# Pooled attention with mixture-of-adapters: another order for the first batch's keys and scores

## The chip, the cores and the metric

The kernel runs on one core of a Trainium2 chip. The core has five engines that run side by side, each through its own list of instructions in order: TensorE (PE) multiplies matrices and transposes tiles, and writes its results to PSUM; VectorE (DVE), ScalarE (ACT) and GpSimd (POOL) work element by element; SyncE (SP) issues transfers (DMAs). An engine that needs another's result waits on a semaphore, and what stands behind the waiting instruction waits too. The metric is the device time of one execution in microseconds (us). The kernel before takes 426.56 us (median of 8 runs, 426.06 to 428.17).

## The reference

There are four batches, each with 12288 queries of 128 channels and a map of 384 x 32 x 128. The map is averaged over patches of 4 x 4 and projected, which gives 768 keys, used as the values too. Each query attends over them. Each row of the result goes through two of eight small adapters, weighted by a softmax over its two largest gate logits, and the sum is added to it.

```python
kv_pool = kv.reshape(B, H // r, r, W // r, r, C).mean(axis=(2, 4))
k = v = kv_pool.reshape(B, -1, C) @ w_sr
s = scale * (q @ k.transpose(0, 2, 1))
a = softmax(s)
x = a @ v                          # 49152 rows of 128
logits = x @ w_gate                # 8 experts, the best two kept
out = x + sum_e w_e * ((x @ A[e]) @ B[e])
```

## The kernel before

**Tiles.** Queries are taken in chunks of 512 (`T`), numbered 0 to 95 over all batches; four chunks make a group of 2048 (`GC`, `GT`). A batch's 768 keys are six tiles of 128 (`J`), treated as three key blocks of two tiles each (`h` or `r` = 0, 1, 2). For each chunk `k` and key block `r`, `scores(k, r)` (L238) multiplies the two key tiles with the chunk's transposed queries (512 columns each) into one of two PSUM buffers (`ps_s`, tile `sg`), and ScalarE takes the exponential of both at once, 128 x 1024 (L246, tile `em`). `attend(k, s)` (L248) multiplies the exponentials with the values (`vx`, which carry the gate's logits and a column of ones beside the 128 channels) into `acc`: 24 matmuls for a chunk. `normalize`, `top`, `route`, `gates`, `transposes`, `down`, `gate`, `up` and `finish` do the rest for a chunk, and `finish` stores it.

**The loop.** From step `k` = 4 (`LA`, L422) on, each step computes the scores of chunk `k`, attends for earlier chunks (table `att`) and passes still earlier ones through the adapters. The next batch's map is loaded and pooled meanwhile, with the additions on GpSimd (L171). Query groups 2 and later are cast to bf16 by a transfer from POOL's queue (`cast_q`) and loaded transposed (`load_qT`, issued by SP).

**The head.** Before the loop stands what the first batch needs (L372 to L390): its keys and values, and the scores of chunks 0 to 3. Query groups 0 and 1 are loaded as they are and transposed on TensorE, four pieces of 128 x 128 to a chunk (`turn_q`, L107), and copied out by ScalarE (L116). A block of the map is loaded in eight pieces of 256 KB: rows `r` = 0 to 3 of the patches, and two halves `x` (each half becomes one key tile). DVE adds rows 0 and 1 and rows 2 and 3 (`pair_step`, L173, recorded as L175). The rest of the sum is made by TensorE: 16 transposes of 128 x 128 accumulate in PSUM (`keys`, L187, tile `kpT_ps`). DVE scales them out (L200, `kpT`), TensorE projects (`keys2`, tile `kfT_ps`) and DVE copies the keys out (L207, `kfT`). `values` (L209) projects the same `kpT` to the values, copied by DVE (L216).

**What sets the order.** The order on every engine is the order in the program's text, as all calls are wrapped in `keep`. Transposes, projections and values share two PSUM buffers (`ps_m`). SP issues all loads in order: the 1 MB of query group 0, then the 24 pieces of the map, then query group 1 in four pieces and the adapters' matrices. On POOL the casts of the query groups 2 and 3 wait for the last piece of group 1 (`late`, L393). In the head TensorE gets: all 16 query transposes of group 0; block 0's keys; scores (0,0) and (1,0); then for each further block its transposes, scores of chunks 2 and 3 with the block before, the projection, the values of the block before, and scores of chunks 0 and 1 with the new block. The last scores are (2,2) and (3,2); then come the first four query transposes of group 1 (L400) and, as the loop's first work, attention of chunk 0 (L448) and scores (4,0).

Every matrix instruction goes through the helper `mm` and so is recorded as L68; the tiles' names tell them apart.

Of the kernel before, what the change touches and what calls it, by code (L numbers as in the profile page):

```python
# [20 lines left out]
def kernel(  # L21
# [10 lines left out]
    nc = tc.nc  # L32
# [92 lines left out]
    load_q(0, 0, GC * S)  # L125
    for h in range(3):
        for r in range(4):
            for x in range(2):
                load_kv(0, h, r, x)
    for m in range(GC):  # L130
        load_q(1, m * S, m * S + S)
# [26 lines left out]
    def prepare(b, adder):  # L158
# [3 lines left out]
        def pool_step(h, step, lo, hi):  # L162
# [3 lines left out]
            else:  # L166
                w = 2 * C if step == 3 else C
                u, v = t[:, 0, :, 0:w], t[:, 0, :, w:2 * w]
                keep(adder.tensor_tensor(u, u, v, op=ALU.add))
                return  # L170
            keep(adder.tensor_tensor(u[:, lo:hi], u[:, lo:hi], v[:, lo:hi], op=ALU.add))  # L171

        def pair_step(h, r, x):  # L173
            u, v = (kvr[b, h][:, r + i, x] for i in range(2))
            keep(adder.tensor_tensor(u, u, v, op=ALU.add))  # L175

        for h in range(3):
            if adder is nc.vector:
                sums.append([lambda h=h, r=r, x=x: pair_step(h, r, x)
                             for r in (0, 2) for x in range(2)])  # L180
                continue
            sums.append([lambda h=h, step=step, lo=lo: pool_step(h, step, lo, lo + 512)
                         for step in range(5) for lo in range(0, 1024 if step < 3 else 512, 512)])
# [3 lines left out]
        def keys(h):  # L187
# [5 lines left out]
            if adder is nc.vector:  # L193
                parts = [(r, i, c) for r in (0, 2) for i in range(2) for c in range(4)]
            else:
                parts = [(0, i, 0) for i in range(2)]
            for n, (r, i, c) in enumerate(parts):
                mm(ps[:, i], kvr[b, h][:, r, i, c * C:(c + 1) * C], id_f, is_transpose=True,
                   start=(n == 0), stop=(n == len(parts) - 1))
# [3 lines left out]
        def keys2(h):  # L203
            kpT = st["kpT"]
            ps = mtile([P, 2, P], name="kfT_ps")
            mm(ps, w_sr_sb, kpT[:, 2 * h:2 * h + 2], start=True, stop=True)
            keep(nc.vector.tensor_copy(kfT[b][:, 2 * h:2 * h + 2], ps))  # L207

        def values(h):  # L209
            if h == 0:  # L210
                vx[b] = per_b.tile([P, J, VE], FP16, tag="vx", name="vx")
                keep(nc.vector.memset(vx[b][:, :, VC:VE], 1.0))
            ps = mtile([P, 2, VC], name="v_ps")
            for i in range(2):
                mm(ps[:, i], st["kpT"][:, 2 * h + i], wext, start=(i == 0), stop=(i == 1))
            keep(nc.vector.tensor_copy(vx[b][:, 2 * h:2 * h + 2, 0:VC], ps))  # L216
            if adder is not nc.vector:
                st["vb", h] = prep.tile([P, 2, C], BF16, tag="vb", name="vb")
                keep(nc.vector.tensor_copy(st["vb", h], ps[:, :, 0:C]))
# [8 lines left out]
        for h in range(3):  # L228
            for f in (keys, keys2, values) if adder is nc.vector else (keys, values, turn):
# [142 lines left out]
    for m in range(GC):  # L372
        turn_q(0, m, nc.scalar)
    sums, rest = prepare(0, nc.vector)
    for h in range(3):
        for item in sums[h]:
            item()
        rest[3 * h]()
        if h > 0:
            scores(2, h - 1)  # L380
        rest[3 * h + 1]()
        if h > 0:
            scores(3, h - 1)
            rest[3 * h - 1]()
        scores(0, h)
        scores(1, h)
    rest[8]()
    scores(2, 2)
    scores(3, 2)
    rest = []  # L390
# [31 lines left out]
    for k in range(LA, last + 3):  # L422
# [10 lines left out]
        if b + 1 < B:  # L433
            if i == 4:
                sums, rest = prepare(b + 1, nc.gpsimd)
# [99 lines left out]
```

The softmax here doesn't subtract the row's maximum and nothing guards it: scores larger than these inputs give would overflow.

## Time and profile before

| | |
|---|---|
| median of 8 runs | 426.56 us (426.06 to 428.17) |
| the profiled execution | 425.39 us, of which the profile's span is 423.3 us |
| TensorE busy | 389.5 us, 92% of the span |
| VectorE, ScalarE, GpSimd busy | 327.3, 292.9 and 162.5 us |
| first exponential of the head | starts at 15.24 us |
| first exponential of loop step 4 | starts at 31.57 us |
| ScalarE's exponentials | 288 of 1.02 us each |
| mean rate of the DMAs | 181 GB/s; 393 to 397 GB/s from 6 to 24 us |

How to read it: the page gives for each engine its busy time and its share of the span, then the span in 40 slices with a digit for the busy tenths of each. The chain of work that ended last is followed back from the last instruction, at each step to what released it, and its time is shared out by engine. The timeline lists instructions in order of time with start and length in us from the start of the span, `xN` where N alike ones were merged (the length is then that of all of them), and in brackets how long the engine was idle before and what ended that. Matmuls overlap: the next starts before the last has drained.

### The profile page before, as it was taken

To read this page: it belongs to the slowest core of one execution; us is meant where nothing else is said; L and a number is where in the kernel's file an instruction comes from. 1 tells how busy PE (TensorE), PEld (TensorE's weight loads), DVE (VectorE), ACT (ScalarE), POOL (GpSimd) and SP (SyncE) were. 2 spreads that over 40 slices of the span, in tenths; PEclk is the share of its full clock that TensorE was granted. 3 is DMA by queue.
4 is the path that set the end of the run, shared out by engine and by line. 5 is a ranking of instruction groups with operands and counts; after the bars stand their busy time and mean duration, and the time that the engine had idled before them with its cause. 6 is when DMAs were issued, how large, how long until landed. Compare 5 with 4: busy or idle time off the path is not lost.

```text
span 423.3 us, 11396 instructions
## 1 busy us (share of the span) xinstructions
PE 389.5 (92%) x4589; PEld 309.8 (73%) x4589; DVE 327.3 (77%) x967; ACT 292.9 (69%) x336; POOL 162.5 (38%) x263
## 2 busy tenths in 40 slices
PE   4898999999999999999999999999999998999843
PEld 3566777787877878787888778777888877788642
DVE  2644778788988878779888878779888888888853
ACT  3478567686777777676787777676777866678522
POOL 0010357965320557964330467963231312222000
PEclk9999999999999999999999999999999999999975
DMA  8989657776547999976547999966584628341112
GB/s 302 404 207 265 136 174 204 272 160 141 130 120 158 286 229 296 294 162 129 145 122 149 316 245 223 323 149 148 128 172 129 150 76 153 131 118 74 53 60 91
DMA packets 71172, 76.43 MB, mean 181 GB/s; under 512 B 49904, under 2 KB 50160, under 8 KB 70640
## 3 DMA queue, kind: packets, MB, share of 16 engines
q1 hardware_dynamic: 70128, 64.11, 52.2%
q0 software_dynamic: 704, 11.54, 15.4%
q8 instruction: 36, 0.59, 0.6%
q14 instruction: 16, 0.13, 0.1%
q10 hardware_dynamic: 288, 0.07, 0.1%
HBM read 50.53 MB, written 36.70 MB: 206 GB/s over the span
## 4 chain that ended last, share of the span: by engine, by line
PE 72%; DVE 10%; POOL 8%; ACT 3%; DMA 2%; issue 2%; SPq 1%; DVEq 0%; ACTq 0%
PE acc L68 28%; PE sg L68 23%; PE tt_ps L68 9%; PE h_ps L68 4%; PE d_ps L68 4%; POOL kvr L171 4%; DVE hg L350 3%; ACT em L246 2%; DVE osb L363 2%; DVE xn L263 2%; POOL over L293 1%; PE v_ps L68 1%; DMA kvr<-in_kv_dram 1%; DMA qf<-in_q_dram 1%; SPq L98 1%
## 5 line engine op out<-in xcount | busy, mean ns | idle before, releaser
L246 ACT ACTIVATE em<-sg 128x1024 f16<-128x1024 f32 x288 | 280.5, 1023 | 97.3 <-PE sg L68 96.4
L68 PE MATMUL acc<-vx,em 128*128 128x137 f16 x2304 | 174.5, 225 | 2.0 <-DVE xn L263 1.9
L68 PE MATMUL sg<-qT,kfT 128*128 128x512 bf16 x576 | 170.9, 378 | 2.7 <-ACT em L246 2.2
L68 PEld LDWEIGHTS <-em 128*128 128x128 f16 x2304 | 150.3, 98 | 4.9 <-DVE xn L263 2.2
L68 PEld LDWEIGHTS <-tts 128*128 128x128 bf16 x768 | 58.7, 99 | 53.1 <-ACT tts L334 5.5
L350 DVE TENSOR_TENSOR hg<-h_ps,gw 128x512 bf16<-128x512 f32 x96 | 66.1, 689 | 29.9 <-POOL gw L315 16.1
L293 POOL TENSOR_TENSOR over<-xn,srt 128x128 f32<-128x128 f32 (+1 forms) x54 | 19.7, 384 | 175.7 <-DVE srt L281 175.7
L263 DVE TENSOR_TENSOR xn<-acc,rinv 128x544 f32<-128x544 f32 x96 | 69.6, 725 | 3.3
L171 POOL TENSOR_TENSOR kvr<-kvr 128x512 f32<-128x512 f32 x54 | 67.4, 1268 | 2.1 <-PE d_ps L68 1.9
L363 DVE TENSOR_TENSOR osb<-d_ps,xn 128x512 f32<-128x512 f32 x96 | 65.9, 690 | 2.6 <-PE d_ps L68 2.6
L336 DVE COPY tts<-tt_ps 128x1024 bf16<-128x1024 bf16 (+1 forms) x95 | 64.0, 673 | 2.4 <-PE tt_ps L68 2.4
L68 PEld LDWEIGHTS <-xn 128*128 128x128 bf16 x384 | 29.5, 99 | 28.5 <-issue 6.1
L68 PEld LDWEIGHTS <-kfT 128*128 128x128 bf16 x576 | 45.9, 97 | 6.0 <-issue 3.7
L68 PE MATMUL h_ps<-a_bf,tts 128*128 128x128 bf16 x384 | 37.6, 221 | 6.1 <-ACT tts L334 3.9
L68 PE MATMUL tt_ps<-id_bf,xn 128*128 128x128 bf16 x384 | 37.4, 220 | 6.1 <-DVE hg L350 4.4
L258 DVE RECIPROCAL rinv<-acc 128x4 f32<-128x4 f32 x96 | 17.4, 181 | 32.8 <-PE acc L68 32.1
L68 PE MATMUL tt_ps<-id_bf,hg 128*128 128x128 bf16 x384 | 37.9, 222 | 3.2 <-DVE hg L350 2.8
L68 PE MATMUL d_ps<-b_bf,tts 128*128 128x128 bf16 x384 | 37.6, 222 | 2.8 <-DVE hg L350 1.2
L281 DVE MAX8 srt<-xn 128x8 f32<-128x8 f32 x384 | 34.6, 153 | 0.2
L68 PEld LDWEIGHTS <-hg 128*128 128x128 bf16 x384 | 25.9, 99 | 4.2 <-DVE hg L350 3.7
L312 ACT ACTIVATE th<-over 128x128 f32<-128x128 f32 (+2 forms) x33 | 9.1, 276 | 15.2 <-DVE over L298 11.8
L314 POOL TENSOR_TENSOR gw<-th,over 128x128 f32<-128x128 f32 (+1 forms) x27 | 11.0, 407 | 21.6 <-ACT th L312 21.5
(49 smaller groups left out, 164.5 us busy)
## 6 DMA issues: line engine op xcount, KB each, us to landing
out_dram<-osb SPq DMA_DIRECT2D x96, 256.0 KB, 3.4
kvr<-in_kv_dram SPq DMA_DIRECT2D x36, 512.0 KB, 6.6
qbf<-in_q_dram POOLq DMA_DIRECT2D x22, 512.0 KB, 7.2
kvr<-in_kv_dram SPq DMA_DIRECT2D x24, 256.0 KB, 5.1
qf<-in_q_dram SPq DMA_DIRECT2D x1, 1024.0 KB, 5.1
qf<-in_q_dram SPq DMA_DIRECT2D x4, 256.0 KB, 5.2
qT<-qbf SPq DMA_TRANSPOSE x22, 8.3
w_sr_sb<-in_w_sr_dram ACTq DMA_DIRECT2D x1, 64.0 KB, 4.0
```

Source lines behind the costliest of these rows:

```text
L68: return keep(nc.tensor.matmul(*a, **k))
L171: keep(adder.tensor_tensor(u[:, lo:hi], u[:, lo:hi], v[:, lo:hi], op=ALU.add))
L246: keep(nc.scalar.activation(em[k][:, 2 * r:2 * r + 2], ps, AF.Exp, bias=0.0, scale=scale))
L258: keep(nc.vector.reciprocal(ri, acc[k][:, :, VC]))
L263: keep(nc.vector.tensor_tensor(x, acc[k][:, :, 0:VC], ri.unsqueeze(2).broadcast_to([P, S, VC]), op=ALU.mult))
L281: keep(nc.vector.max(srt[k0][:, m, s], xn[k][:, s, C:VC]))
L293: keep(eng.tensor_tensor(d, lg, so[:, :, i].unsqueeze(2).broadcast_to([P, n, 8]), op=ALU.subtract))
L312: keep(nc.scalar.activation(th, arg, AF.Tanh, bias=0.0, scale=0.5))
L314: keep(eng.tensor_tensor(w[:, 0:n], th, mask, op=ALU.mult))
L336: keep(nc.vector.tensor_copy(sb[:, lo:hi], ps[:, lo:hi]))
L350: keep(nc.vector.tensor_tensor(hg[k].rearrange("p s (e r) -> p (s e) r", e=E), hp[k].rearrange("p s (e r) -> p (s e) r", e=E), gw[k0][:, m ...
L363: keep(nc.vector.tensor_tensor(osb, dp[k], xn[k][:, :, 0:C], op=ALU.add))
```

## The change

The loop is left as it is. What changes is the head. Query group 0 is loaded in two halves of 512 KB, with the eight pieces of block 0 between them. The pieces of each block are loaded half by half (`x` outside, `r` inside). The scores are taken block by block: all four chunks with block 0, then with block 1, then with block 2. Query chunks 2 and 3 are transposed between the scores of block 0. Block 2 is built in two columns, one key tile each, with scores of chunks 2 and 3 of block 1 between them; in its second column rows 2 and 3 aren't added by DVE, but both transposed into the sum by TensorE (four transposes more, one addition less). The attention of chunk 0 moves from the loop's first step to a place ahead of scores (3,2). `prepare` loses its branches for the first batch; for the other batches it does what it did.

```diff
-    load_q(0, 0, GC * S)
+    load_q(0, 0, 2 * S)
     for h in range(3):
-        for r in range(4):
-            for x in range(2):
+        for x in range(2):
+            for r in range(4):
                 load_kv(0, h, r, x)
+        if h == 0:
+            load_q(0, 2 * S, 4 * S)
...
+    def values_of(b, h, kpT):
...
+        ps = mtile([P, 2, VC], name="v_ps")
+        for i in range(2):
+            mm(ps[:, i], kpT[:, 2 * h + i], wext, start=(i == 0), stop=(i == 1))
+        keep(nc.vector.tensor_copy(vx[b][:, 2 * h:2 * h + 2, 0:VC], ps))
+        return ps
...
-    for m in range(GC):
-        turn_q(0, m, nc.scalar)
-    sums, rest = prepare(0, nc.vector)
-    for h in range(3):
-        for item in sums[h]:
-            item()
-        rest[3 * h]()
-        if h > 0:
-            scores(2, h - 1)
-        rest[3 * h + 1]()
-        if h > 0:
-            scores(3, h - 1)
-            rest[3 * h - 1]()
-        scores(0, h)
-        scores(1, h)
-    rest[8]()
-    scores(2, 2)
-    scores(3, 2)
-    rest = []
+    def pair(h, x, r):
+        u, v = (kvr[0, h][:, r + i, x] for i in range(2))
+        keep(nc.vector.tensor_tensor(u, u, v, op=ALU.add))
+
+    def patches(ps, h, x, rs, first_, last_):
+        n = [(r, c) for r in rs for c in range(4)]
+        for i, (r, c) in enumerate(n):
+            mm(ps, kvr[0, h][:, r, x, c * C:(c + 1) * C], id_f, is_transpose=True,
+               start=(first_ and i == 0), stop=(last_ and i == len(n) - 1))
+
+    def pooled(ps, lo, hi):
+        keep(nc.vector.tensor_scalar(kpT0[:, lo:hi], ps, 1.0 / 16.0, None, op0=ALU.mult))
+
+    def project(lo, hi):
+        ps = mtile([P, 2, P], name="kfT_ps")[:, 0:hi - lo]
+        mm(ps, w_sr_sb, kpT0[:, lo:hi], start=True, stop=True)
+        keep(nc.vector.tensor_copy(kfT[0][:, lo:hi], ps))
+
+    def both(h):
+        ps = mtile([P, 2, P], name="kpT_ps")
+        for x in range(2):
+            for r in (0, 2):
+                pair(h, x, r)
+                patches(ps[:, x], h, x, (r,), x == 0 and r == 0, x == 1 and r == 2)
+        pooled(ps, 2 * h, 2 * h + 2)
+        project(2 * h, 2 * h + 2)
+
+    turn_q(0, 0, nc.scalar)
+    turn_q(0, 1, nc.scalar)
+    both(0)
+    scores(0, 0)
+    scores(1, 0)
+    values_of(0, 0, kpT0)
+    turn_q(0, 2, nc.scalar)
+    scores(2, 0)
+    turn_q(0, 3, nc.scalar)
+    scores(3, 0)
+    both(1)
+    scores(0, 1)
+    scores(1, 1)
+    pair(2, 0, 0)
+    pair(2, 0, 2)
+    ps = mtile([P, P], name="kpT_ps")
+    patches(ps, 2, 0, (0, 2), True, True)
+    pooled(ps, 4, 5)
+    scores(2, 1)
+    values_of(0, 1, kpT0)
+    project(4, 5)
+    scores(3, 1)
+    pair(2, 1, 0)
+    ps = mtile([P, P], name="kpT_ps")
+    patches(ps, 2, 1, (0, 2, 3), True, True)
+    pooled(ps, 5, 6)
+    project(5, 6)
+    scores(0, 2)
+    scores(1, 2)
+    values_of(0, 2, kpT0)
+    scores(2, 2)
+    for s in range(S):
+        attend(0, s)
+    scores(3, 2)
...
         if k == LA:
-            for s in range(S):
-                attend(0, s)
             ka = []
```

## The prediction

> **What bounds the kernel now.** I read the page first (busy shares, slices, chain), then the timeline of the first 50 us, where the change lies, then the waits. The page:
>
> ```profile
> PE 389.5 (92%) x4589; PEld 309.8 (73%) x4589; DVE 327.3 (77%) x967; ACT 292.9 (69%) x336; POOL 162.5 (38%) x263
> ...
> PE   4898999999999999999999999999999998999843
> ...
> PE 72%; DVE 10%; POOL 8%; ACT 3%; DMA 2%; issue 2%; SPq 1%; DVEq 0%; ACTq 0%
> ...
> kvr<-in_kv_dram SPq DMA_DIRECT2D x24, 256.0 KB, 5.1
> qf<-in_q_dram SPq DMA_DIRECT2D x1, 1024.0 KB, 5.1
> ```
>
> TensorE is full except in the first slices and the last, and carries 72% of the chain. So what the head (the first batch's keys, up to the loop) gains or loses goes on to the end one for one, if nothing later stands at a fixed time. The head, in the timeline (start, length, engine, line, what; in brackets the idle time before it and who ended it):
>
> ```profile
> 6.52 3.74 PE L68 MATMUL qT_ps<-id_f,qf 128*128 128x128 f32 x16
> ...
> 10.69 1.41 DVE L175 TENSOR_TENSOR kvr<-kvr 128x512 f32<-128x512 f32 x2 [1.18 <-DMA kvr<-in_kv_dram]
> 12.84 0.43 DVE L200 TENSOR_SCALAR kpT<-kpT_ps 128x256 f32<-128x256 f32 x1 [0.75 <-PE kpT_ps L68]
> ...
> 14.12 0.42 DVE L207 CAST kfT<-kfT_ps 128x256 bf16<-128x256 f32 x1 [0.85 <-PE kfT_ps L68]
> ...
> 14.60 1.04 PE L68 MATMUL sg<-qT,kfT 128*128 128x512 bf16 x4 [0.52 <-DVE kfT L207]
> 15.24 1.94 ACT L246 ACTIVATE em<-sg 128x1024 f16<-128x1024 f32 x2 [4.36 <-PE sg L68]
> ...
> 15.47 1.04 PE L68 MATMUL kpT_ps<-id_f,kvr 128*128 128x128 f32 x8
> 16.10 1.47 DVE L175 TENSOR_TENSOR kvr<-kvr 128x512 f32<-128x512 f32 x2 [0.36 <-DMA kvr<-in_kv_dram]
> ...
> 18.32 0.42 DVE L200 TENSOR_SCALAR kpT<-kpT_ps 128x256 f32<-128x256 f32 x1 [0.75 <-PE kpT_ps L68]
> ...
> 19.97 2.85 ACT L246 ACTIVATE em<-sg 128x1024 f16<-128x1024 f32 x3 [0.19 <-PE sg L68]
> ```
>
> and its end:
>
> ```profile
> 25.67 4.69 ACT L246 ACTIVATE em<-sg 128x1024 f16<-128x1024 f32 x5 [0.19 <-PE sg L68]
> ...
> 29.44 1.66 PE L68 MATMUL acc<-vx,em 128*128 128x137 f16 x24
> 30.21 0.63 ACT L116 CAST qT<-qT_ps 128x512 bf16<-128x512 f32 x1
> ...
> 30.94 0.59 PE L68 MATMUL sg<-qT,kfT 128*128 128x512 bf16 x2
> ...
> 31.57 1.02 ACT L246 ACTIVATE em<-sg 128x1024 f16<-128x1024 f32 x1 [0.73 <-PE sg L68]
> ```
>
> Key block 0 waits for its loads (DVE until 10.69). From 15 us on ScalarE's exponentials set the pace, 0.92 apart when nothing stops them. They stop where a key block isn't ready:
>
> ```profile
> ACT em L246 <- PE sg L68: 8.0, 5, 4.4
> ```
>
> (ScalarE's waits from 14 to 31 us: 8.0 us in five waits, of which 4.4 before the first exponential.) The mark that I carry through is the first exponential of step 4, the loop's first: it starts at 31.57. TensorE reaches its scores, 30.94, when the copy of 30.21 to 30.84 is done, since that copy holds the queries of step 4.
>
> **The change, step by step.** I write e(k,r) for the exponential of query chunk k and key block r. On each engine instructions run in order.
>
> *Loads.* Only half of the 1 MB of queries now lies ahead of block 0's eight loads. The DMAs move 405 GB/s in the windows from 8 us on: 0.52 MB is 1.3 us; at the 302 to 370 GB/s of 2 to 6 us it would be 1.4 to 1.7, and 1.0 is the least if SP's issues (0.60 each, L98) are what paces the first ones. I take 1.3. Block 0's last two additions end at 12.10 - 1.3 = 10.8. The second half goes behind block 0, so blocks 1 and 2 land as before, and SP issues one DMA more (0.40): the loads of the next query group and of the adapters are issued up to 0.4 later, but the bytes before them are the same. The POOL copy that waits for them (24.57), the casts behind it in POOL's queue and the transposing load behind those in SP's (30.52) stay, or slip by at most 0.4; the tile that they make is used at step 8, more than 20 us later, which hides it. Column by column, an addition now needs loads 1 and 2, then 3 and 4: it costs nothing, the last one decides.
>
> *Block 0.* TensorE turns 8 query pieces first, not 16: 6.52 + 8 x 0.23 = 8.4. The 16 transposes of the keys follow the additions. At 0.107 a start (15.47: 8 in 1.04) the last four end 0.75 after the last addition, 11.55; if all still run at 0.23 a start, as the row at 6.52 does, 8.4 + 3.7 = 12.1. I take 11.9. From that copy to the first exponential it is 15.24 - 12.84 = 2.4: e(0,0) at 14.3, a gain of 0.95.
>
> *Block-major scores.* Now TensorE's order is scores 0, scores 1, values, turn query chunk 2, scores 2, turn chunk 3, scores 3, and only then the transposes of block 1. ScalarE's is e(0,0) 14.3, e(1,0) 15.2, copy of chunk 2 at 16.1 to 16.7. Scores 2 wait for that copy: 16.75, and their exponential follows 0.63 later (30.94 to 31.57), 17.4. Chunk 3 is turned behind scores 2, so its copy stands behind e(2,0): 18.3 to 18.9; scores 3 at 18.95, e(3,0) at 19.6. All that while block 1's transposes are queued behind scores 2 and 3 on TensorE. They start at 18.95 + 0.43 = 19.4, though their additions are done by 17.8 (the values' copy of 0.45 moves ahead of them on DVE; it is covered by this wait). Sixteen of them and the drain take 2.0: kpT at 21.4, where it was 18.32. Plus 2.4: e(0,1) at 23.8, where it was 20.89. The gain of 0.95 has become a loss of 2.9. ScalarE is idle from 20.6.
>
> *Block 2 by columns, with the last rows on TensorE.* Two additions behind block 1's copy on DVE (from 23.1, 0.6 apart) end at 24.4; four transposes to 25.1; kpT, 128x128, costs 0.29 (the nearest row is L150's 128x128 copy, 0.29; ends 0.17 for 128x8 and 0.43 for 128x256). Scores (2,1), values, the half projection and scores (3,1) follow: e(3,1) at 26.8. On DVE the values' copy (26.05 to 26.5) and the half key copy come before the one addition left: 26.7 to 27.4. Then 12 transposes (8 of rows that are no longer added, 4 in place of an addition of 0.69) to 28.9, kpT 0.29, half projection 0.45 (ends 0.35, as the 136-column values matmuls run, and 0.70, the whole one), copy 0.29, scores: e(0,2) at 30.7. Before it was 25.67 + 0.92 = 26.6, so the loss is 4.1. The last loads land near 22 (two loads per 1.35 us after 16.1), so the additions that went are no wait that ended: nothing stands on them any more.
>
> *Attention moved up.* The 24 matmuls (1.5) now stand ahead of scores 3, not behind them. e(1,2) 31.6, e(2,2) 32.5, attention 32.2 to 33.7, scores (3,2) 33.7, e(3,2) 34.35 instead of 33.45: 0.9 more, since ScalarE has nothing else. Then as before the copy of step 4's queries (35.25), scores at 35.9 and e of step 4 at 36.5. Normalising chunk 0 moves less (+2.7), but its products sit in ScalarE's queue behind step 4 and gain nothing.
>
> *Sum:* -0.95 + 3.85 (block-major) + 1.2 (columns) + 0.8 (attention) = 36.5 - 31.57 = +4.9. The unknown prices (half load 0.4 either way, clock 0.3, five narrow operations 0.1 each) make it +3.7 to +6.1. The profiled execution took 425.39 (span 423.3 and 2.1 around it), so 430.3; the median of the runs, 426.56, is 1.2 above it, and gives 431.5. A difference under 0.2%, 0.9 us, can't be told from none.
>
> **The clock of the transposes.** The transposes at 6.52 start 0.23 apart and those at 15.47 about 0.11, with the granted clock at 1.00 in both windows, so something halves TensorE's rate that the clock row doesn't show. In the new order TensorE has 8 query transposes fewer early on and idles more between 12 and 30 us. What it does on the path there at full rate is 36 transposes (3.9), seven score pairs (3.0), projections (1.1) and the attention (1.5), 9.5 us; if the full rate came after the head, the loss would be 4.9 + 9.5 = 14.4 us. If it came by 15 us, in place of some 11.5, it would cost about 1.2 more, by 18 us about 2.2 more.
>
> The Trainium skill, "TensorE: Matmul & The Clock Gate", Part 1, says that the array runs at half rate until one window of about 3.4 us has been busy, and falls back after an idle one; that speaks against this change. Its Part 4 says that transposes do not count as such activity. The rows contradict Part 4: between 6.52 and 12.8 us only transposes ran, and they sped up. By Part 1, with the near unbroken transposes from 6.5 to 11.9, the sum stays at +4.9; by Part 4 the first half of the head would be at half rate and the sum 6 to 7.
>
> **The rivals.** *The clock comes later* (above): 432.7 to 433.7, at worst 441. For it: fewer early transposes, four TensorE pauses of 0.6 to 1.5 us. Against: additions and transposes keep TensorE at work until about 12.
>
> *The loop absorbs the delay.* If the loop's start stood at a fixed time, that of next batch's loads or of POOL's additions (POOL has 8% of the chain), up to 4.9 us would vanish and the time be 426.6, no change. It decides if that slack is 4.9 or more. Against: after 24.6 no wait on a DMA is in the list of waits; POOL waits for DVE (175.7 us), ScalarE and TensorE, which all move along.
>
> *The change does what its order aims at,* and ScalarE runs through: twelve exponentials and two copies from 14.3 give step 4 at 27.7, 3.9 earlier, 422.7. It decides if block 1's keys are turned by 18, that is if TensorE isn't held at scores 2 and 3. Against: both wait for copies that stand behind exponentials.
>
> **How the numbers follow.** Forecast, +3.7 to +5.5: 0.72. Clock later: 0.15. Absorbed: 0.07. ScalarE through: 0.06. Range 429.6 to 433.8: from 0.8 below the low end of the sum, for slack that takes a little of it, to the clock at 18 us; it leaves out the last two cases and the clock's far end. Faster 0.06 (ScalarE through), same 0.05 (absorbed in full), slower 0.89 (the rest, with 0.02 for absorbed in part).
>
> **What would show it.** Exponentials of block 0 at about 14.3, 15.2, 17.4 and 19.6 with two query copies between; block 1's kpT copy near 21.4; ScalarE idle some 3 us before e(0,1) and again before e(0,2); step 4's first exponential near 36.5; the rows from 50 us on the same, later. It is wrong if block 1's transposes start before 18, if transposes are still 0.2 apart after 15 us, or if the delay at 36 us is smaller at 100.

## The result, and the profile after

The changed kernel takes 432.08 us (median of 11 runs) and the kernel before 426.56 us; the ratio is 1.0131, with a 95% interval of 1.0113 to 1.0148. It is slower by about 5.5 us. The ratio and its interval leave out executions in a slower state that any of these kernels now and then falls into (one of the eleven, at 442.84 us; the other ten took 430.94 to 434.99). The profiled execution took 431.16 us with a span of 429.2, against 425.39 and 423.3 before: 5.8 us more.

The page of the changed kernel, with the lines that answer to those shown of before (busy time by engine, TensorE's slices, the granted clock by slice, the chain that ended last, the query load):

```profile
PE 390.7 (91%) x4595; PEld 311.2 (73%) x4595; DVE 327.1 (76%) x968; ACT 293.1 (68%) x336; POOL 162.7 (38%) x263
...
PE   4677999999999999999999999999999998999853
...
PEclk9999999999999999999999999999999999999955
...
PE 69%; DVE 10%; POOL 9%; DMA 5%; ACT 3%; issue 2%; SPq 1%; ACTq 0%; DVEq 0%
...
qf<-in_q_dram SPq DMA_DIRECT2D x2, 512.0 KB, 5.7
```

TensorE's work is the same within 1.2 us. Its slices 2 to 4 fell from 898 to 677: the time was lost in the head, as idle time of TensorE. The chain's share of DMA rose from 2% to 5%, but this is no wait: the chain is followed back at 26.74 from a copy on VectorE to the landing of the adapters' `a_f`, which that copy does not read, and VectorE was busy with the copy ahead of it until 26.83. ScalarE's timeline of the head shows where (start, length, idle time before in brackets):

```profile
14.82 1.94 ACT L233 ACTIVATE em<-sg 128x1024 f16<-128x1024 f32 x2 [5.65 <-PE sg L68]
16.65 0.59 ACT L116 CAST qT<-qT_ps 128x512 bf16<-128x512 f32 x1
17.92 1.02 ACT L233 ACTIVATE em<-sg 128x1024 f16<-128x1024 f32 x1 [0.68 <-PE sg L68]
18.84 0.58 ACT L116 CAST qT<-qT_ps 128x512 bf16<-128x512 f32 x1
20.10 1.02 ACT L233 ACTIVATE em<-sg 128x1024 f16<-128x1024 f32 x1 [0.68 <-PE sg L68]
24.18 3.88 ACT L233 ACTIVATE em<-sg 128x1024 f16<-128x1024 f32 x4 [3.06 <-PE sg L68]
30.95 2.85 ACT L233 ACTIVATE em<-sg 128x1024 f16<-128x1024 f32 x3 [2.89 <-PE sg L68]
34.58 1.02 ACT L233 ACTIVATE em<-sg 128x1024 f16<-128x1024 f32 x1 [0.77 <-PE sg L68]
35.50 0.58 ACT L116 CAST qT<-qT_ps 128x512 bf16<-128x512 f32 x1
36.76 1.02 ACT L233 ACTIVATE em<-sg 128x1024 f16<-128x1024 f32 x1 [0.68 <-PE sg L68]
```

Each of ScalarE's pauses is put down to scores of TensorE. The two copies in block 0 are followed by pauses of 0.68; before the first exponential of block 1 it waits 3.06, before that of block 2 2.89. The exponential of step 4 starts at 36.76, where it was 31.57: 5.19 later. From there every exponential up to step 94 stays 5.19 to 5.22 later, so the loop neither absorbs nor adds anything. Behind the last exponential 0.64 more is added, which makes the 5.86 between the two spans. The timeline of TensorE and VectorE of the changed kernel shows what holds block 1:

```profile
19.47 0.59 PE L68 MATMUL sg<-qT,kfT 128*128 128x512 bf16 x2 [1.15 <-ACT qT L116]
19.54 0.69 DVE L364 TENSOR_TENSOR kvr<-kvr 128x512 f32<-128x512 f32 x1 [0.61 <-DMA kvr<-in_kv_dram]
19.90 1.91 PE L68 MATMUL kpT_ps<-id_f,kvr 128*128 128x128 f32 x16
...
21.84 0.42 DVE L373 TENSOR_SCALAR kpT<-kpT_ps 128x256 f32<-128x256 f32 x1 [1.61 <-PE kpT_ps L68]
```

TensorE waits 1.15 us for a query copy, does scores (3,0), and only then, at 19.90, turns block 1's keys; the copy-out of `kpT` starts at 21.84, before it was 18.32. The last addition of block 1 too ends late, at 20.23 (19.54 + 0.69; before 17.57), but the transposes have 12 other pieces to turn until then.

### The profile page after: what moved, and what is told of

Same layout as the page of the kernel before. It is cut to its first block, busy times and chain, and to the rows that moved or that the text cites. A ratio compares the mean times of both kernels' runs of the same rounds, so it can differ in the third digit from the quotient of the medians.

```text
span 429.2 us, 11412 instructions
## 1 busy us (share of the span) xinstructions
PE 390.7 (91%) x4595; PEld 311.2 (73%) x4595; DVE 327.1 (76%) x968; ACT 293.1 (68%) x336; POOL 162.7 (38%) x263
## 4 chain that ended last, share of the span: by engine, by line
PE 69%; DVE 10%; POOL 9%; DMA 5%; ACT 3%; issue 2%; SPq 1%; ACTq 0%; DVEq 0%
PE acc L68 27%; PE sg L68 22%; PE tt_ps L68 8%; PE d_ps L68 4%; PE h_ps L68 4%; POOL kvr L183 4%; DMA kvr<-in_kv_dram 3%; DVE hg L337 3%; DVE osb L350 2%; POOL over L280 2%; DVE xn L250 2%; ACT em L233 2%; PE v_ps L68 1%; SPq L98 1%; DVE tts L323 1%
## 5 line engine op out<-in xcount | busy, mean ns | idle before, releaser
L301 POOL TENSOR_TENSOR gw<-th,over 128x128 f32<-128x128 f32 (+1 forms) x27 | 11.0, 406 | 21.6 <-ACT th L299 21.5
```

The costliest lines, as they stand in the source:

```text
L301: keep(eng.tensor_tensor(w[:, 0:n], th, mask, op=ALU.mult))
```

## The experiments

My theory was the sum of the prediction: block-major order, columns and attention each cost what their waits show, and the two query halves cost nothing by themselves. The rivals were that part of the loss is TensorE's clock, which the sparser order keeps or loses, or the loads, which the second half of the queries pushes back. All times below are medians; each ratio is to executions of the kernel before that were made beside it (their medians are 426.24 to 426.86).

| kernel | us | ratio to before, interval | step 4's exponential in its profile, later than 31.57 by |
|---|---|---|---|
| the changed kernel | 432.08 | 1.0131 (1.0113 to 1.0148) | 5.19 |
| `half_alone` | 428.18 | 1.0046 (1.0031 to 1.0062) | 3.34 |
| `halves_ahead` | 426.54 | 0.9996 (0.9979 to 1.0012) | 0.48 |
| `attend_back` | 431.03 | 1.0124 (1.0078 to 1.0171) | 8.2 |
| `block2_whole` | 430.82 | 1.0100 (1.0079 to 1.0120) | 6.47 |
| `dve_copies` | 431.78 | 1.0134 (1.0101 to 1.0166) | 6.56 |
| `after_warm` | 431.15 | 1.0108 (1.0093 to 1.0123) | 5.37 |
| `block2_whole_warm` | 430.00 | 1.0073 (1.0055 to 1.0090) | 4.16 |
| `dve_copies_warm` | 430.44 | 1.0089 (1.0073 to 1.0106) | 4.66 |
| `half_warm` | 428.62 | 1.0053 (1.0025 to 1.0081) | 3.62 |
| `before_warm` | 427.51 | 1.0037 (1.0020 to 1.0054) | 0.98 |
| `whole_first` | 430.12 | 1.0081 (1.0055 to 1.0107) | 3.68 |
| `between` | 426.44 | 0.9995 (0.9980 to 1.0011) | 0.31 |

The last column is of single executions. In `half_alone`, `attend_back`, `block2_whole` and `dve_copies` that execution ran part of the head at half the clock; the medians say more there.

### The halves alone

`half_alone` is the kernel before with the query load cut in two around block 0, and chunks 2 and 3 turned after the scores of block 0:

```diff
-    load_q(0, 0, GC * S)
+    load_q(0, 0, 2 * S)
...
+        if h == 0:
+            load_q(0, 2 * S, 4 * S)
...
-    for m in range(GC):
+    for m in range(2):
         turn_q(0, m, nc.scalar)
...
         scores(1, h)
+        if h == 0:
+            for m in range(2, GC):
+                turn_q(0, m, nc.scalar)
```

> The kernel before with one part of the change: the queries in two halves around block 0, query chunks 2 and 3 transposed behind the first two scores of block 0; the loads otherwise, the order of the scores, block 2 and the attention as before. My theory (the half load brings block 0 forward by about 0.5 to 1 us, but the later blocks still wait for their own loads): the first exponential near 14.3 to 14.8 instead of 15.24, step 4 at 31.6 within 0.6, time 426 to 427.2. Rival (the second half slows the loads of block 1 and 2, which in the changed kernel landed some 1.7 us later than before): block 1's last addition ends near 19 to 20 instead of 17.57, step 4 at 33 or later, time 427.8 to 429.

It is slower by 0.46%, 2.0 us, so "no change" fell, and the rival's time of 427.8 to 429 came true. But the rival's reason did not show: block 1's last addition ended at 18.09, not at 19 to 20. In its profile TensorE ran at the half rate until 20.4 us, which its timeline shows by the lengths:

```profile
15.30 1.89 PE L68 MATMUL sg<-qT,kfT 128*128 128x512 bf16 x4 [0.52 <-DVE kfT L209]
16.98 1.92 PE L68 MATMUL qT_ps<-id_f,qf 128*128 128x128 f32 x8
18.84 2.72 PE L68 MATMUL kpT_ps<-id_f,kvr 128*128 128x128 f32 x16
21.40 0.59 PE L68 MATMUL sg<-qT,kfT 128*128 128x512 bf16 x2
```

Four score matmuls take 1.89 at 15.30, where before they took 1.04. Its transposes of block 1 started at 18.84, behind the turned queries.

`halves_ahead` cuts the load too, but puts both halves ahead of the map:

```diff
-    load_q(0, 0, GC * S)
+    load_q(0, 0, 2 * S)
+    load_q(0, 2 * S, 4 * S)
```

> The kernel of before with the 1 MB of queries cut in the same two halves, both still ahead of block 0; nothing else. In the profiles with the second half behind block 0 it took 0.8 to 2.4 us to land where 0.52 MB at 405 GB/s take 1.3, and all later loads came 0.5 to 1.8 later. Theory A (halves of 4 KB a partition are slow themselves): the second half lands at 6.0 or later (before: all at 5.5), block 0's last addition ends after 12.4, step 4 later by as much, time 427 to 428. Theory B (a half is slow only among the pieces of the map): landing at 5.5 within 0.3 and time 426.6 within 0.5.

The medians tell no difference: two loads in place of one cost nothing that this measurement can tell. (In its profile block 0's last addition ended at 12.61, beyond the 12.4 of theory A; but so it did with one whole load, at 12.86 in `between` and 12.78 in `before_warm`.) So what costs in `half_alone` is where the second half goes, and what TensorE then does when.

### The attention of chunk 0

`attend_back` puts it back into the loop's first step:

```diff
     scores(2, 2)
-    for s in range(S):
-        attend(0, s)
     scores(3, 2)
...
         if k == LA:
+            for s in range(S):
+                attend(0, s)
             ka = []
```

> The changed kernel with the attention of chunk 0 back behind scores (3,2), where it was before. My theory: the exponential (3,2) follows (2,2) again without a pause (33.7 instead of 34.58), step 4 starts 0.8 earlier, near 36.0; time 0.8 below the changed kernel's, about 431.3. Rival (the attention has to be done anyway and only changes places): no difference, 432.1 within 0.3.

The median is 1.0 us below the changed kernel's, but the interval of its ratio holds the changed kernel's 1.0131, so the time alone does not settle it. The mechanism can be read directly. In ScalarE's timeline of `attend_back` the last four exponentials of the head run through:

```profile
34.79 3.77 ACT L233 ACTIVATE em<-sg 128x1024 f16<-128x1024 f32 x4 [2.89 <-PE sg L68]
...
39.77 1.02 ACT L233 ACTIVATE em<-sg 128x1024 f16<-128x1024 f32 x1 [0.73 <-PE sg L68]
```

They start about 0.92 apart, where the changed kernel has three, a pause of 0.77 and the fourth (30.95 and 34.58 above). From block 2's first exponential to that of step 4 it is 4.98 here, as before (26.59 to 31.57), and 5.81 in the changed kernel. The attention ahead of scores (3,2) costs these 0.83; every profile with it there has 5.80 or 5.81.

### Block 2 in two columns

`block2_whole` is the changed kernel with block 2 in one piece, in the order of before; `block2_whole_warm` is the same with transposes that feed nothing in the pauses (they are explained below).

```diff
-    pair(2, 0, 0)
-    pair(2, 0, 2)
-    ps = mtile([P, P], name="kpT_ps")
-    patches(ps, 2, 0, (0, 2), True, True)
-    pooled(ps, 4, 5)
+    ps = mtile([P, 2, P], name="kpT_ps")
+    for x in range(2):
+        for r in (0, 2):
+            pair(2, x, r)
+            patches(ps[:, x], 2, x, (r,), x == 0 and r == 0, x == 1 and r == 2)
+    pooled(ps, 4, 6)
     scores(2, 1)
-    values_of(0, 1, kpT0)
-    project(4, 5)
+    project(4, 6)
     scores(3, 1)
-    pair(2, 1, 0)
...
-    project(5, 6)
+    values_of(0, 1, kpT0)
     scores(0, 2)
```

> The changed kernel with block 2 built in one piece, in the order of before (four additions on VectorE, 16 transposes, scores (2,1), projection, scores (3,1), values, scores (0,2)); everything else as changed. My theory (the two columns cost 1.2 us because each goes through VectorE and TensorE by turns): exponential (0,2) at 29.4 instead of 30.95, step 4 near 35.3, time 1.2 to 1.5 lower, 430.6 to 430.9. Rival (four whole additions and the last loads hold it up instead, as the change's last rows on TensorE suppose): no gain or a loss, 432 to 433.

> The kernel with block 2 in one piece, with the extra transposes. My theory (two columns cost 1.2): time 1.2 to 1.5 below the changed kernel with the extra transposes, exponential (0,2) at 29.4 to 29.6. Rival (the 1.3 that the run without extra transposes was below the changed kernel came from the clock): within 0.4 of it.

Both are about 1.2 us below their counterparts with columns (430.82 against 432.08; 430.00 against 431.15). The interval of `block2_whole` overlaps that of the changed kernel, but the four runs of `block2_whole_warm` (429.03 to 430.30) all lie below the four of `after_warm` (430.71 to 431.73). ScalarE's timeline of `block2_whole_warm`, blocks 1 and 2:

```profile
24.91 1.94 ACT L240 ACTIVATE em<-sg 128x1024 f16<-128x1024 f32 x2 [3.06 <-PE sg L68]
27.79 1.02 ACT L240 ACTIVATE em<-sg 128x1024 f16<-128x1024 f32 x1 [0.94 <-PE sg L68]
29.01 3.77 ACT L240 ACTIVATE em<-sg 128x1024 f16<-128x1024 f32 x4 [0.19 <-PE sg L68]
```

In one piece, ScalarE waits 0.94 and 0.19 in the middle of block 1 and then runs on; with columns it does all four of block 1 without a pause and then waits 2.89. From the first exponential of block 1 to that of block 2 it is 6.77 with columns (24.18 to 30.95) and 5.02 in one piece (24.91 to 29.93, the second of the four at 29.01). Of these 1.75 step 4 gains 1.21 in this execution (4.16 late against 5.37 in `after_warm`), since its block 0 began 0.55 later.

### The query copies between the scores

`dve_copies` lets VectorE copy chunks 2 and 3 and turns both ahead of scores (2,0); `dve_copies_warm` is that with the filler.

```diff
-    turn_q(0, 2, nc.scalar)
+    turn_q(0, 2, nc.vector)
+    turn_q(0, 3, nc.vector)
     scores(2, 0)
-    turn_q(0, 3, nc.scalar)
     scores(3, 0)
```

> The changed kernel with the copies of query chunks 2 and 3 on VectorE instead of ScalarE, both chunks transposed ahead of scores (2,0). It takes away what scores (2,0) and (3,0) wait for, the copies behind the exponentials. My theory (that wait holds block 1's transposes): exponentials (2,0) and (3,0) at 17.4 and 18.3 instead of 17.92 and 20.10, block 1's transposes start at 17.8 instead of 19.9; block 1's kpT then follows its last addition (ended 20.24 in the changed kernel's profile) at 20.9 instead of 21.84, and the time falls by 0.9, to 431.2; if the loads come as early as before (last addition 17.6), by 2.5 to 3, to 429. Rival (block 1 is held by its loads alone, not by the order): kpT stays at 21.8, time 432 within 0.4.

> The kernel with the copies of query chunks 2 and 3 on VectorE, with the extra transposes. The run without them lost the clock (half from 12.8 to 19.7 us) and so tells little of the order. My theory (block 1's transposes are held by scores 2 and 3, which wait for copies behind exponentials): exponentials (2,0), (3,0) near 17.4 and 18.3, block 1's kpT 0.75 after its last addition, step 4 at 34.8 to 35.9, time 0.9 to 2 below the changed kernel with the extra transposes. Rival (block 1 is held by its loads): no more than 0.3 below it.

Without the filler it gains nothing that can be told (431.78). With it, it is 0.7 below `after_warm`, less than the 0.9 to 2 expected, and the two sets of four runs overlap. VectorE's timeline of `dve_copies_warm` tells why it is not more:

```profile
16.72 1.45 DVE L118 CAST qT<-qT_ps 128x512 bf16<-128x512 f32 x2
18.08 2.49 DVE L371 TENSOR_TENSOR kvr<-kvr 128x512 f32<-128x512 f32 x4
21.32 0.42 DVE L380 TENSOR_SCALAR kpT<-kpT_ps 128x256 f32<-128x256 f32 x1 [0.75 <-PE kpT_ps L68]
```

The four additions of block 1 now stand behind the copies on VectorE, and block 1's keys are out at 21.32 in place of 21.84: the wait moved from ScalarE's copies to VectorE's additions.

`whole_first` takes the copies out of the way on ScalarE itself: the queries are loaded whole, ahead of the map, and all four chunks are turned first. The block-major order stays, with nothing between the scores.

```diff
-    load_q(0, 0, 2 * S)
+    load_q(0, 0, 4 * S)
...
-        if h == 0:
-            load_q(0, 2 * S, 4 * S)
...
     turn_q(0, 1, nc.scalar)
+    turn_q(0, 2, nc.scalar)
+    turn_q(0, 3, nc.scalar)
     both(0)
...
-    turn_q(0, 2, nc.scalar)
     scores(2, 0)
-    turn_q(0, 3, nc.scalar)
     scores(3, 0)
```

> The changed kernel with the 1 MB of queries in one load ahead of block 0 and all 16 query transposes and their copies ahead of block 0's keys, as before; the column-wise loads, the block-major scores without copies between them, block 2 in columns and the early attention stay. My theory (most of the block-major loss comes from the two copies and transposes between the scores, the rest from block 1's transposes behind scores 2 and 3): first exponential at 15.2, exponentials 2 and 3 at 17.1 and 18.0, block 1's transposes start at 17.7, exponential (0,1) at 22.0 (changed kernel 24.18, before 20.89), step 4 at 34.6, time 429.4 to 429.9. Rival (the copies don't matter, block-major order alone does it): exponential (0,1) stays near 24 and the time near 431 to 432.

430.12 us, 2.0 below the changed kernel and a little above the 429.4 to 429.9 expected. ScalarE's timeline of `whole_first`, blocks 0 and 1:

```profile
15.85 3.77 ACT L231 ACTIVATE em<-sg 128x1024 f16<-128x1024 f32 x4 [4.40 <-PE sg L68]
22.68 3.88 ACT L231 ACTIVATE em<-sg 128x1024 f16<-128x1024 f32 x4 [3.06 <-PE kfT_ps L68]
```

From block 0's first exponential to block 1's it is 6.83 here, 9.36 in the changed kernel (14.82 to 24.18) and 5.65 before (15.24 to 20.89). So of the 3.71 that the block-major order lost there, 2.53 is the two copies standing among the exponentials, and 1.18 is the order of the blocks itself. (The loads of block 1 came earlier here too, but in the changed kernel its keys did not wait for them.) Where the 1.18 comes from, VectorE's timeline of `whole_first` shows:

```profile
17.10 2.49 DVE L362 TENSOR_TENSOR kvr<-kvr 128x512 f32<-128x512 f32 x4
```

The four additions of block 1 follow the copy of block 0's values (16.74 to 17.19), which waits for TensorE behind the scores. They end at 19.59, before at 17.57, though the last piece of the block had landed at 17.26. In the changed kernel the wait for the query copies covers this; without the copies it is the next wait. About 1.0 of the 2.53 is given back at the start, since block 0 begins at 15.85 and not at 14.82.

### The clock

`after_warm` is the changed kernel with transposes of the identity into an accumulator that nothing reads, 16 at the start and 2 to 8 in the pauses. They feed nothing and only keep TensorE at work:

```diff
+    def fill(n):
+        for _ in range(n):
+            mm(scratch[:, 0, 0:P], id_f, id_f, is_transpose=True, start=True, stop=True)
+
+    fill(16)
...
     turn_q(0, 2, nc.scalar)
+    fill(8)
     scores(2, 0)
     turn_q(0, 3, nc.scalar)
+    fill(8)
     scores(3, 0)
```

> The changed kernel with extra transposes of the identity into an unused accumulator, 16 ahead of everything else on TensorE and 2 to 8 in each of its pauses in the head; they feed nothing. It keeps TensorE busy and moves no other work. My theory (in a part of the executions of the changed kernel the clock falls back to half in the pauses of the head, and that is the distance of its median from its best runs): no granted clock of 0.5 before 400 us, step 4 at 36.8 or a little earlier, time 430.4 to 431.2 with a spread under 1 us, against 432.08 with 430.9 to 435.0. Rival (the spread comes from the loads): median and spread stay, 432 within 0.4.

Its median is 0.9 us below the changed kernel's (431.15 against 432.08), though it does more, and its four runs lie within about 1 us (430.71 to 431.73). But the intervals of the two ratios overlap, so the 0.9 is not secured. In its profile the clock is full from 10.21 us to 409.6, and step 4 is 5.37 late, filler included; the profile of the changed kernel kept the clock too and has 5.19. This is the price of the order with the clock out of the question.

What the clock adds where it is lost can be read from the distance between the first exponentials of block 0 and block 1: it is 9.36 in the changed kernel, `after_warm` and `block2_whole_warm`, and 11.72 and 11.45 in the profiles of `attend_back` and `block2_whole`, whose clock fell twice in the head. Whether this is what spreads the changed kernel's runs (430.94 to 434.99) is not shown. Of every execution the mean granted clock is on record: in `attend_back` it goes with the time (0.968 at 434.27 and 0.973 at 431.67, 0.976 at 430.38 and 430.39); in the changed kernel the three slowest of the ten (433.08, 433.23, 434.99) have 0.975, 0.982 and 0.975, and the three fastest 0.975 to 0.979.

`half_warm` is `half_alone` with filler, and `before_warm` is the kernel before with the filler of block 0, as a control:

```diff
+                if b == 0 and h == 0 and n in (3, 7, 11):
+                    fill({3: 2, 7: 8, 11: 2}[n])
+            if b == 0 and h == 0:
+                fill(4)
...
+            if h == 0:
+                fill(3)
```

> The kernel of before with the half load alone, with the extra transposes. The run without them was 1.3 above before, with the clock at half until 20.4 us. Theory A (the half load costs by the clock alone: fewer early transposes): first exponential near 14.3, step 4 at 31.6 to 32.1, time 426.3 to 427.2, no slower than before. Theory B (it costs by its loads too, which come 0.5 later for block 1): 427 to 427.8. Rival (the clock has nothing to do with it): 428.2 again.

> The kernel before, with the transposes that feed nothing put into block 0 in the same manner as in after_warm (16 first, 2 to 8 behind pieces of block 0, 4 and 3 around its projection). It is the control for after_warm, which came out 0.9 us below after's median. If that 0.9 is the price of the clock that the changed order loses, then the kernel before, whose profile shows the full clock without a break from 11.65 us to 404 us, can gain little: its block 0 waits for loads until 12.10 us, and 426.3 to 426.7, no difference, is expected. If the filler helps any order alike, the kernel before gains too and comes to about 425.6. If the fillers themselves are in the way (each 0.1 to 0.2 us ahead of real work), it is 0.2 to 0.5 us slower.

The control got slower by 1.3 us: in its profile block 0's last addition ended 0.7 later than in the profile of before (12.78 against 12.09; the two starts differ, see below), and filler stood 0.35 in the way of the last transposes. The filler isn't free in a head that waits for loads.

`half_warm` is 1.1 above `before_warm`, but their intervals overlap. At 428.62 it lies above what both theories allowed, near the rival's 428.2. Its profile settles that the loads can cost by themselves. The clock is full from 11.53 us on, and VectorE's timeline of `half_warm` shows block 1 waiting for its pieces:

```profile
16.33 1.39 DVE L184 TENSOR_TENSOR kvr<-kvr 128x512 f32<-128x512 f32 x2 [1.55 <-DMA kvr<-in_kv_dram]
18.92 1.40 DVE L184 TENSOR_TENSOR kvr<-kvr 128x512 f32<-128x512 f32 x2 [1.19 <-DMA kvr<-in_kv_dram]
```

The last addition ended at 20.32 (before at 17.57), the keys' copy-out followed 0.74 later, and step 4 was 3.62 late. In the profile of `half_alone` it was the clock and the query transposes ahead of block 1's keys: the additions ended only 0.5 later than before. How much of the 2.0 in the runs of `half_alone` is which stays open.

What goes with a loss of the clock can be read in the profiles. It is granted in periods of 3.41 us. The three views that follow are stretches of one such period each (from and to, length, busy time of PE, PEld, DVE, ACT, POOL, then PEclk, DMA share, GB/s). First `attend_back`, which lost the clock twice, here the first time:

```profile
11.73:15.14 3.41, 1.33 (x6) 0.72 (x6) 1.51 (x3) 0.00 (x0) 0.00 (x0) 1.00 1.01 366
15.14:18.56 3.42, 3.33 (x12) 2.41 (x13) 0.57 (x4) 1.94 (x2) 0.00 (x0) 0.50 1.05 393
```

Then the changed kernel, in the profiled execution:

```profile
11.77:15.18 3.41, 2.28 (x12) 1.29 (x13) 0.88 (x3) 0.36 (x1) 0.00 (x0) 1.00 1.02 352
15.18:18.59 3.41, 1.97 (x15) 1.42 (x14) 2.08 (x4) 2.73 (x4) 0.00 (x0) 1.00 0.99 370
18.59:22.01 3.42, 2.34 (x18) 1.90 (x17) 1.20 (x3) 1.85 (x3) 0.00 (x0) 1.00 1.01 371
```

And the kernel before:

```profile
11.65:15.06 3.41, 2.28 (x15) 1.41 (x15) 1.81 (x5) 0.00 (x0) 0.00 (x0) 1.00 1.05 404
15.06:18.47 3.41, 2.95 (x21) 2.02 (x19) 2.22 (x5) 1.94 (x2) 0.00 (x0) 1.00 1.05 406
```

A period at full clock with TensorE busy 1.33 us is followed by one at half (3.33 busy there, since each matmul takes twice as long). Over the heads of all these profiles, full periods with 1.33 to 1.97 us busy were followed by half ones, nine of them (four of these in profiles with filler, ahead of 8.4 us), and none with 2.05 or more was; the changed kernel's 1.97 at 15.18 is the only one in that border that stayed full. In the profile of before no period of the head from 11.65 us on has less than 2.28. The new order lies at the border, so it can depend on where the periods fall in an execution whether it loses any. That this share, and nothing that goes with it, decides was not tested by itself, and the busy times are modelled, so the border may be off by a tenth.

### The same aim without the pauses

`between` keeps the old order and puts scores between the transposes of the next block, sums the last rows of block 2 on TensorE and makes the values late:

```diff
+        for i, (r, x) in enumerate([(0, 0), (0, 1), (2, 0), (2, 1)]):
+            if i == 2:
+                scores(2, h - 1)
+            if (r, x) in lasts:
+                turned(r, x)
+                turned(r + 1, x)
+            else:
+                sums[h][i]()
+                turned(r, x)
...
+        scores(3, h - 1)
         rest[3 * h + 1]()
         scores(0, h)
...
+    block(1, [])
+    scores(1, 1)
+    block(2, [(2, 1)])
+    rest[2]()
+    scores(1, 2)
+    rest[5]()
     rest[8]()
```

> Before's order with what the runs leave of the change: the last two rows of block 2 both transposed into the sum by TensorE (one addition less), scores (2,r) between block r+1's transposes instead of behind them, scores (3,r) ahead of the projection, and the values copied after block 2's keys instead of ahead of its additions; queries loaded whole. My theory (what counts is when the next block's keys are done, 25.67 before): kpT of block 2 at 23.5 instead of 24.03, exponential (0,2) 0.5 to 0.8 earlier than 26.59, step 4 near 30.8 to 31.0, time 0.5 to 0.8 below before, 425.8 to 426.1. Rival (block 2 waits for its last loads anyway): within 0.3 of before.

426.44 us: no difference. ScalarE's timeline of `between`, its twelve exponentials of the head:

```profile
16.19 2.85 ACT L246 ACTIVATE em<-sg 128x1024 f16<-128x1024 f32 x3 [4.51 <-PE sg L68]
19.23 1.02 ACT L246 ACTIVATE em<-sg 128x1024 f16<-128x1024 f32 x1 [0.19 <-PE sg L68]
21.14 2.86 ACT L246 ACTIVATE em<-sg 128x1024 f16<-128x1024 f32 x3 [0.89 <-PE sg L68]
24.62 1.02 ACT L246 ACTIVATE em<-sg 128x1024 f16<-128x1024 f32 x1 [0.62 <-PE sg L68]
26.53 1.94 ACT L246 ACTIVATE em<-sg 128x1024 f16<-128x1024 f32 x2 [0.89 <-PE sg L68]
28.78 1.94 ACT L246 ACTIVATE em<-sg 128x1024 f16<-128x1024 f32 x2 [0.32 <-PE sg L68]
```

The pauses behind the first are now under 0.9 each, and block 2's first exponential comes 10.34 after block 0's (before 11.35, from 15.24 to 26.59). But this execution began its exponentials 0.95 later, and the end of the head gave 0.3 back at 28.78. From the first exponential to step 4 it is 0.64 less than before, which the medians do not show. The time is what the rival said; its reason isn't seen, as VectorE waited only 0.17 for the loads of block 2. No version that was run is faster than the kernel before.

## Why the prediction was right, and where its steps were off

The prediction was 431.5 us and slower; it is 432.08, inside the range of 429.6 to 433.8 (whose low end is 0.7 below that of the sum, 430.3, and not 0.8). The mechanism was the one that it named, and its terms, measured up to the mark of step 4's first exponential:

| term | predicted | measured |
|---|---|---|
| block 0 | -0.95 (first exponential 14.3) | -0.42 (14.82) |
| block-major scores | +3.85 (block 1's at 23.8) | +3.71 (24.18; 9.36 after block 0's, before 5.65) |
| columns | +1.2 (block 2's at 30.7) | +1.07 (30.95; 6.77 after block 1's, before 5.70) |
| attention | +0.8 (step 4 at 36.5) | +0.83 (36.76) |
| sum | +4.9 | +5.19 |
| end of the run | nothing | +0.7 (not of the change, see the clock) |

**Block 0** was the term that was mis-sized, with "I take 1.3" for the half load. The last additions of block 0 ended at 11.66, not 10.8; the load that went out of the way was worth 0.43 in this pair of profiles, not 1.3. Two executions differ by more than that there. In five kernels with all queries ahead of block 0 (the kernel before, `halves_ahead`, `between`, `before_warm`, `whole_first`) the last addition ended between 12.09 and 12.86, middle 12.61, and the profile of the kernel before is the earliest of them; in the nine with half of them ahead it ended between 11.42 and 12.72, middle 11.79. By the middles the half load is worth 0.8. Part of the miss cancelled by luck: the prediction took 1.1 from the last addition to the copy-out of `kpT`, between its values for the full and the half rate, and it was 0.76, as at the full rate.

**Block-major scores, columns and attention** each came within 0.15, and each was undone alone: without the copies among the scores the kernel is 2.0 faster, with block 2 in one piece 1.2 faster, with the changed kernel's ratio outside their intervals; with the attention back the pause of 0.77 is gone, with 1.0 in the medians that the interval does not secure. The distances between the marks say it more sharply than the medians, as they hardly vary: block 1 to block 2 is 6.77 in all six kernels with columns and 5.02 in the two without, and block 2 to step 4 is 5.80 or 5.81 in the seven with the early attention. The signs named beforehand were there: block 1's `kpT` at 21.84 (said: near 21.4), ScalarE idle 3.06 and 2.89 (said: some 3), the same delay at step 94.

**"Blocks 1 and 2 land as before" was wrong.** The last piece of the map landed at about 24.6 instead of 22.0, block 1's last addition ended 2.7 later, and the transposing load of SP went from 30.52 to 33.50, where the prediction allowed 0.4. None of it is on the path in this kernel: TensorE had no time for block 1's keys until 19.90 anyway, and after 36 us there is no wait for a DMA in its list. It isn't what holds `dve_copies_warm` either: there the last piece of block 1 landed at 18.61, and the addition that needs it started at 19.88, behind the copies and the other additions. It is on the path in `half_warm`, as shown above. What came late is the second half. The DMAs of the changed kernel moved less while it was in flight, in stretches of 2 us (columns as above):

```profile
8.00:10.00 2.00, 2.00 (x11) 1.78 (x10) 1.31 (x2) 0.90 (x2) 0.00 (x0) 1.00 0.99 344
10.00:12.00 2.00, 1.47 (x9) 1.07 (x8) 0.69 (x1) 0.00 (x0) 0.00 (x0) 1.00 0.90 254
12.00:14.00 2.00, 1.05 (x6) 0.44 (x4) 0.73 (x2) 0.00 (x0) 0.00 (x0) 1.00 1.00 332
```

Before it was 405, 395 and 409 GB/s in the same stretches. In the changed kernel the half landed at 14.28, 7.2 after its issue and 3.4 after the piece before it. In `half_alone` and `dve_copies` it was 1.3 after that piece, which is what 0.52 MB take at 405 GB/s, and in the six others 2.0 to 3.7 (so the 0.8 to 2.4 in the expectation of `halves_ahead` was misread). With both halves ahead of the map it is 1.3 too. Why it is slow in some executions was not tried and stays open.

**The clock** was made a rival of its own, 432.7 to 433.7 at 0.15, with the question by when the full rate comes. It came in time, at 11.77 in the profile; but it can be lost again, which the prediction did not price (2.1 and 2.4 in the profiles of `block2_whole` and `attend_back`). That the 0.9 between `after_warm` and the changed kernel, or its spread, comes from this is possible and not shown. Of the five profiles with the second half behind block 0 and no filler, four had the half rate for 6.8 us of the head, or until 20.4; only that of the changed kernel itself did not. The clock also goes with the 0.7 at the end. The end of the kernel before, in the same periods:

```profile
404.18:407.60 3.42, 2.74 (x25) 2.74 (x26) 1.47 (x3) 0.63 (x1) 0.00 (x0) 0.50 0.20 77
407.60:411.01 3.41, 1.48 (x20) 1.01 (x17) 1.39 (x3) 1.01 (x1) 0.00 (x0) 1.00 0.00 0
411.01:414.42 3.41, 1.04 (x8) 0.77 (x8) 2.73 (x13) 1.01 (x2) 0.00 (x0) 0.50 0.44 161
```

And after the change:

```profile
404.30:407.71 3.41, 1.63 (x23) 1.22 (x21) 2.71 (x8) 1.04 (x2) 0.00 (x0) 1.00 0.15 57
407.71:411.12 3.41, 1.89 (x16) 1.61 (x16) 2.55 (x13) 1.13 (x2) 0.00 (x0) 0.50 0.02 8
411.12:414.53 3.41, 2.49 (x23) 2.22 (x20) 0.29 (x1) 0.88 (x1) 0.00 (x0) 0.50 0.18 69
414.53:417.95 3.42, 1.62 (x12) 1.20 (x12) 2.48 (x5) 0.13 (x1) 0.00 (x0) 0.50 0.15 53
```

Before, one full period lies among the half ones (407.60); after, there is none. `after_warm`, which has one again (413.0 to 416.4), has no extra 0.7 at its end: it ends 5.33 later than before, with 5.37 at step 4. The other profiles say that this is where the periods fall, and no cost of the change. From the start of the last exponential to the end it is 24.83 to 24.88 us in nine of the fourteen profiles, the changed kernel's and the old order's `halves_ahead` and `before_warm` among them, and 24.13 to 24.45 in five. Four of the five, the kernel before among them, are the profiles with a full period among the half ones; in the fifth, `dve_copies`, the half clock began only 17.8 us ahead of the end, in the others 18.6 to 21.5.

The prediction weighed the Trainium skill, "TensorE: Matmul & The Clock Gate", Part 1, for falling back after an idle window. The rows agree with its window of about 3.4 us (3.41 here), but the windows after which the clock fell were not idle: TensorE was busy for 39 to 58% of them.

**The other rivals.** The loop absorbed nothing (5.19 at step 4, 5.22 at step 94). Of the kernels with block-major scores only `whole_first` let ScalarE run through block 0, and there block 1 was the next wait, 3.06 long.

## What to carry to other kernels

An order that gives one engine long runs without a wait is paid for by the engine that prepares the next block: here TensorE's transposes of the next keys stood behind scores that waited for copies queued behind exponentials. When work is moved, follow each engine's queue past the moved instruction, and ask which wait was hiding the next. And count how busy TensorE stays: an order that leaves it near half busy in the head can cost the clock on top of the waits.

## What the runs showed of the hardware

- The clock's fall goes with the share of a 3.41 us period in which TensorE was busy, with a border of about 1.9 to 2.05 us in these profiles, not with one long idle stretch: the longest single pause in the nine periods that lost it was 0.74 to 1.49 us, and the changed kernel kept it through a pause of 1.17. Coming up took more: half periods with 2.73 to 3.41 us busy were followed by full ones, one with 2.62 was not (`dve_copies`, 12.84 to 16.25), nor one with 2.90 in `half_alone` (13.60 to 17.02), so that border is not sharp.
- Until the first entry of an execution's clock record the row of the granted clock reads 1.00, though TensorE runs at half: in `half_alone` until 20.43 us. There the start-to-start time of alike instructions has to be read: 0.11 us for a 128 x 128 fp32 transpose at the full rate and 0.23 at the half.
- Executions differ at the very start: the additions of block 0 in kernels with the same loads ahead of them ended up to 0.77 us apart. A gain of half a microsecond in the head can't be read from where a mark stands in a single profile. Distances between two marks of one execution repeat far better: within 0.01 us for those of block 1 to block 2 and of block 2 to step 4 in the kernels with block-major scores and the same order from there on.
